# Gated recurrence and bilinear feed-forward: blocks of four token tiles, two PSUM banks for the up-projections

## The chip, the cores and the metric

One core of a Trainium2 chip runs the whole program in one launch. The metric is the device time of one execution in microseconds (us), lower being better. The core's engines are called here by the profile's names: PE (TensorE, the matmuls; its loading of weights is shown as PEld), DVE (VectorE), ACT (ScalarE), POOL (GpSimd) and SP (SyncE, whose queue issues the DMAs). TensorE writes its results to PSUM, which has eight banks; a bank holds 512 float32 values in each of 128 partitions.

## The reference

There are 4 sequences (B), 8 heads (H), 768 steps (S) and 40 values per head (D). For each step and head a matrix state C and a vector state n are updated under two gates with a running maximum, and read with q. The result is the input x of a bilinear feed-forward layer: 3072 tokens, 320 wide, 1536 inner columns, everything in float32.

```python
m_new = np.maximum(f_gate[:, :, t] + m, i_gate[:, :, t])
f_stab = np.exp(f_gate[:, :, t] + m - m_new)
i_stab = np.exp(i_gate[:, :, t] - m_new)
C = f_stab[..., None, None] * C + i_stab[..., None, None] * np.einsum('bhd,bhe->bhde', vt, kt)
n = f_stab[..., None] * n + i_stab[..., None] * kt
h_tilde = np.einsum('bhde,bhe->bhd', C, qt)
denom = np.maximum(np.abs(np.einsum('bhd,bhd->bh', n, qt)), 1.0)[:, :, None]
y[:, :, t] = sigmoid(o_gate[:, :, t]) * h_tilde / denom
...
x = y.transpose(0, 2, 1, 3).reshape(B * S, H * D)
out = ((x @ w_a) * (x @ w_b)) @ w_out
```

## The kernel before

**Attention.** The recurrence is computed in chunks of 128 steps, so there are 24 tiles of 128 tokens, six for each sequence; tile n is chunk n // 4 of sequence n % 4. For a tile, `stage_a` (or `begin_a`) turns q and k so that heads lie along partitions, `stage_e`/`begin_e` make the matrix of gate factors, `stage_b` multiplies it with the scores (PSUM tile pS), `stage_i` reads the state left by earlier chunks (pI), `stage_c` applies the weights to v (pV), `stage_u` updates the state (pU), `stage_f` divides and applies the output gate, and `stage_d` transposes the result (pX) and leaves it as x in two parts: xh, the value rounded to the matmul's format, and xl, what the rounding left. Tiles 0 to 5 use the float32 forms (`begin_...`), the others sums of bfloat16 parts.

**Feed-forward.** `moe_block` takes a block of consecutive tiles together. For each of 12 slices of 128 inner columns (ff), `up` fills two PSUM accumulators, acc[0] = x w_a and acc[1] = x w_b, with eight matmuls each (three parts of the contraction; high and low parts of weights and of x). The matmuls are as wide as the block: 128 columns a tile (L693). ACT copies acc[0] to g (L699; DVE does it in slices 1 and 2), DVE multiplies acc[1] by g (L700), rounds the product to gh (L702), and gl is what the rounding left (L704). `down(ff)` adds gh and gl times w_out into one PSUM accumulator pd for each tile, three matmuls a tile (L664), and runs two slices behind `up`: in a block's first two slices no `down` stands between the `up`s. Behind the last slice ACT copies each pd to o (L673), and SP sends it out (L674). g and o are tiles of one kind, "acp", with three buffers.

**Weights.** The weights arrive as raw 64-bit words. `weights` converts them in 32 stages; `first` makes a high word W and a remainder r with ACT and DVE, and `second` adds them exactly with two matmuls into a PSUM tile pc (L352, L353), from which DVE makes the low part (L354). A block's projections can't run ahead of the stage that they use (`need`). The conversion ends within block 0.

**PSUM.** Three banks "pu" serve acc, and also pc, the gate scores pE of the first tiles and half of the first transposes pT; three banks pd0 to pd2 serve the down-projections (pd2 also pU of tiles 2 to 5, while blocks have two tiles); two banks "pat" serve attention.

**Order.** Each engine works off its instructions in the order in which they are queued. A scheduler sets that order when the program is built, from the order in which the program names the instructions, from simulated times and from the buffers that are free. The program names attention's steps between the projections' matmuls: while block kb is projected, the loop at the end advances attention until the last tile of block kb+1 is done, in steps of a pace (`units / total`). Block 0 may begin when tiles 0 and 1 are done, and each block when all of its tiles are.

The numbers of lines are those of the kernel before.

Of the kernel before, what the change touches and what calls it, by code (L numbers as in the profile page):

```python
# [8 lines left out]
F32 = mybir.dt.float32  # L9
BF16 = mybir.dt.bfloat16  # L10
F32R = mybir.dt.float32r
# [5 lines left out]
PSUM = bass.MemoryType.PSUM  # L17
# [3 lines left out]
def kernel(  # L21
# [14 lines left out]
    B, H, S, D = q.shape  # L36
    DM, DFF = w_a.shape
    P = 128
    NC = S // P
    NF = DFF // P  # L40
    BH = B * H
    DV = D + 2
    TB = 3
    NTB = TB * P
    WCH = 384
    CVB = 8
    STAGES = 8

    BEHIND = ((0, ("k", 0)), (1, ("k", 1)), (14, ("k", 2)), (22, ("k", 3)))
    NF32 = 6  # L50
# [4 lines left out]
    rpool = ctx.enter_context(tc.tile_pool(name="rpool", bufs=1))  # L55
    apool = ctx.enter_context(tc.tile_pool(name="apool", bufs=2))
    dpool = ctx.enter_context(tc.tile_pool(name="dpool", bufs=1, space=bass.MemoryType.DRAM))
    ps_up = ctx.enter_context(tc.tile_pool(name="ps_up", bufs=3, space=PSUM))
    ps_dn = ctx.enter_context(tc.tile_pool(name="ps_dn", bufs=1, space=PSUM))
    ps_at = ctx.enter_context(tc.tile_pool(name="ps_at", bufs=2, space=PSUM))  # L60

# [18 lines left out]
    HH = H // 2  # L80
# [33 lines left out]

    chunks = [(c, b) for c in range(NC) for b in range(B)]
    NCH = len(chunks)
    sizes = [2, 2, 3, 3, 3, 3, 3, 2, 3]
    NB = len(sizes)
    begins = [sum(sizes[:x]) for x in range(NB + 1)]
    assert begins[-1] == NCH and max(sizes) <= TB  # L120
# [61 lines left out]
        return x.bitcast(BF16).rearrange("p h (d w) -> p h d w", w=2)[:, :, :, 1]  # L182

    def gates():
        f = room("g_f")[0:BH, 0:S]
        i = room("g_i")[0:BH, 0:S]
        nc.sync.dma_start(f, f_gate.rearrange("b h s -> (b h) s"))
        nc.sync.dma_start(i, i_gate.rearrange("b h s -> (b h) s"))
        m = room("g_m")[0:BH]
        gb = m[:, S:].rearrange("p (w t) -> p w t", w=2)  # L190
        m = m[:, 0:S]
        yield
# [114 lines left out]
    def weights():  # L307
        stages = list(weight_stages())
        held = {}

        def fetch(x):
            if x < len(stages):
                src = stages[x]
                n = src[0].shape[1]
                raw = rpool.tile([P, n], I64, tag=f"s{x}", name=f"raw{x}")
                r0 = 0
                behind = [y for first, y in BEHIND if x >= first][-1]
                with tc.issue_after(issued[behind]), tc.issue_after(issued.get("w", issued[behind])):
                    for a in src:
                        raw_in = nc.sync.dma_start(raw[r0:r0 + a.shape[0]], a).ins  # L320
                        r0 += a.shape[0]
                issued["w"] = raw_in
                held[x] = [raw, n]

        def first(x):
            raw, n = held[x]
            W = cpool.tile([P, WCH], F32, tag="cv", name="cw", bufs=CVB)[:, :n]
            t = step[x % len(step)][:, :n]
            words = raw.bitcast(U32).rearrange("p (n w) -> p n w", w=2)
            lo, hi = words[:, :, 0], words[:, :, 1]  # L330
            wu, tu = W.bitcast(U32), t.bitcast(U32)


            nc.scalar.activation(t, hi.bitcast(F32), AF.Prelu, scale=2.0 ** -112, alpha=-(2.0 ** 32))
            nc.vector.tensor_scalar(wu, tu, 3, None, op0=ALU.logical_shift_left)
            nc.vector.tensor_scalar(tu, wu, 0xFF800000, None, op0=ALU.bitwise_and)
            r = cpool.tile([P, WCH], F32R, tag="cv", name="cr", bufs=CVB)[:, :n]
            nc.vector.scalar_tensor_tensor(r, lo, 2.0 ** -52, t, op0=ALU.mult, op1=ALU.mult)
            held[x] += [W, r]

        def second(x):

            ready[0] = x + 1
            raw, n, W, r = held.pop(x)
            w = ws[x] = rpool.tile([P, 2, n], F32R, tag=f"s{x}", name=f"w{x}")
            h, l = w[:, 0], w[:, 1]
            last = len(stages[x]) > 1
            if last:
                h, l = (cpool.tile([P, WCH], F32R, tag="ct", name="ct", bufs=2) for _ in range(2))
            nc.scalar.copy(h, W)  # L350
            pc = ps_up.tile([P, NTB], F32, tag="pu", name=f"pc{x}")[:, :n]
            nc.tensor.matmul(pc, eye[0], r, start=True, stop=False)  # L352
            nc.tensor.matmul(pc, eye[1], h, start=False, stop=True)  # L353
            nc.vector.tensor_tensor(l, pc, W, op=ALU.add)  # L354
            if last:
                for j in range(2):
                    rows, other = (slice(64 * i, 64 * i + 64) for i in (j, 1 - j))
                    nc.sync.dma_start(w[rows, j].bitcast(F32), h[rows].bitcast(F32))
                    nc.sync.dma_start(w[other, j].bitcast(F32), l[rows].bitcast(F32))

        fetch(0)
        yield -1
        for x in range(1, 4):
            fetch(x)
        for x in range(len(stages) + 1):
            fetch(x + 4)
            if x < len(stages):
                first(x)
                yield x
            if x > 0:  # L370
                second(x - 1)
                yield x
        for x in qks2:
            for w in range(2):
                nc.gpsimd.memset(x[:, w, :, 3 * D:], 0.0)
# [208 lines left out]
        yield  # L584

    xt = {}

    def stage_d(n):
        s = st.pop(n)
        k_ = block[n]  # L590
        t0 = (n - begins[k_]) * P
        if t0 == 0:
            xt[k_] = (
                mpool.tile([P, 3, NTB], F32R, tag="xh", name=f"xh{k_}", bufs=2),
                mpool.tile([P, 3, NTB], F32R, tag="xl", name=f"xl{k_}", bufs=2),
            )
        xh, xl = xt[k_]
        pX = ps_at.tile([P, 512], F32, tag="pat", name=f"pX{n}")
        for t in range(3):
            nc.tensor.transpose(pX[:, t * P:(t + 1) * P], s["y"][:, t * P:(t + 1) * P], ident)  # L600
        yield
        px = pX[:, 0:3 * P].rearrange("p (a t) -> p a t", a=3)
        cols = slice(t0, t0 + P)
        after["a"] = [nc.scalar.copy(xh[:, :, cols], px).ins]
        nc.vector.tensor_tensor(
            xl[:, :, cols], px, xh[:, :, cols].bitcast(F32), op=ALU.subtract
        )
        yield ("done", n)
# [108 lines left out]
    def begin_e(n):  # L717
# [3 lines left out]
        E = E.rearrange("p (h t) -> p h t", h=H)  # L721
        st.setdefault(n, {})["E"] = E
        for hf in range(2):
            tag = "pu"
            pE = (ps_up if tag == "pu" else ps_at).tile([P, HH, P], F32, tag=tag, name=f"pE{n}_{hf}")
            for x in range(HH):
                one_hot = sel[:, b * H + hf * HH + x:b * H + hf * HH + x + 1].broadcast_to([3 * BH, P])
                nc.tensor.matmul(pE[:, x], one_hot, stk[:, 0], start=True, stop=False)
# [5 lines left out]
    def begin_a(n):  # L734
# [5 lines left out]
        for j in range(2):  # L740
# [3 lines left out]
                t = apool.tile([P, 2 * H * P], BF16, tag=f"T{j}", name=f"T{n}_{j}", bufs=1).bitcast(F32)  # L744
                t = t[:, 0:HH * P].rearrange("p (h t) -> p h t", h=HH)
            T.append(t)
            tag = "pu" if n < NS and j == 1 else "pat"
            pT = (ps_up if tag == "pu" else ps_at).tile([P, 512], F32, tag=tag, name=f"pT{n}_{j}")
            pt = pT.rearrange("p (h t) -> p h t", h=HH)
            for x in range(HH):  # L750
                nc.tensor.transpose(  # L751
# [73 lines left out]

    cpool = ctx.enter_context(tc.tile_pool(name="cpool", bufs=1))
    conv = weights()
    with tc.tile_pool(name="spool", bufs=7) as spool:

        def room(name):  # L830
            return spool.tile([P, H * P], F32, tag="x", name=name)
# [62 lines left out]
    for kb in range(NB):  # L894
# [1 line left out]
        done = False  # L896
        acc = 0.0
        total = NF * (16 + 3 * sizes[kb])
        units = 36 * sizes[kb + 1] if kb + 1 < NB and kb < 2 else 66 * TB
        for x, _ in enumerate(moe_block(kb)):  # L900
            if x % 6 == 0:
                next(conv, None)
# [38 lines left out]
```

## Time and profile before

| | |
|---|---|
| median of 3 runs | 578.44 us (574.6, 578.44, 578.54) |
| span of the profiled execution, first to last instruction | 572.6 us |
| the profiled execution's own time | not given beside its span |
| busy: PE, PEld | 96%, 92% |
| busy: DVE, ACT, POOL | 69%, 46%, 23% |
| granted PE clock, mean | 0.973 |

From the records of L693, 192 for each block, the blocks begin at these times (us from the span's start):

| block | 0 | 1 | 2 | 3 | 4 | 5 | 6 | 7 | 8 |
|---|---|---|---|---|---|---|---|---|---|
| tiles | 2 | 2 | 3 | 3 | 3 | 3 | 3 | 2 | 3 |
| begins | 47.5 | 128.4 | 168.3 | 233.1 | 295.0 | 356.5 | 418.1 | 476.3 | 518.1 |

How to read it: a busy share is of the whole span, and the blocks differ. A matmul's duration in the profile contains its way through the array, so matmuls overlap, and how fast they follow each other is read from their starts. "[1.28 <-DMA out_dram<-o]" behind a row of the order-of-time view says that the engine was idle for 1.28 us before it, and what came last of what it waited for; "x3" says that three instructions in a row were merged.

### The profile page before, as it was taken

To read this page: it belongs to the slowest core of one execution; us is meant where nothing else is said; L and a number is where in the kernel's file an instruction comes from. 1 tells how busy PE (TensorE), PEld (TensorE's weight loads), DVE (VectorE), ACT (ScalarE), POOL (GpSimd) and SP (SyncE) were. 2 spreads that over 40 slices of the span, in tenths; PEclk is the share of its full clock that TensorE was granted. 3 is DMA by queue.
4 is the path that set the end of the run, shared out by engine and by line. 5 is a ranking of instruction groups with operands and counts; after the bars stand their busy time and mean duration, and the time that the engine had idled before them with its cause. 6 is when DMAs were issued, how large, how long until landed. Compare 5 with 4: busy or idle time off the path is not lost.

```text
span 572.6 us, 12609 instructions
## 1 busy us (share of the span) xinstructions
PE 547.5 (96%) x4864; PEld 526.0 (92%) x4864; DVE 396.8 (69%) x884; ACT 265.9 (46%) x634; POOL 129.1 (23%) x182
## 2 busy tenths in 40 slices
PE   3799999999999999999999999999999999999997
PEld 2688999889999989999999999999999899999996
DVE  6866788975578777499649976698648654954342
ACT  3644565673255465255825554555525921411111
POOL 3021331463213222123303330332111200200000
PEclk9857999989999999999999999999999999999999
DMA  9979945365244966267954676478538603200000
GB/s 206 285 184 278 228 111 107 73 153 121 63 103 115 190 118 142 75 123 148 155 109 110 150 150 131 115 159 159 109 97 129 154 2 99 59 2 23 1 2 34
DMA packets 199863, 68.34 MB, mean 119 GB/s; under 512 B 184476, under 2 KB 193084, under 8 KB 199804
## 3 DMA queue, kind: packets, MB, share of 16 engines
q1 hardware_dynamic: 199804, 67.55, 54.6%
q8 instruction: 38, 0.62, 0.5%
q14 instruction: 21, 0.17, 0.1%
HBM read 41.11 MB, written 5.97 MB: 82 GB/s over the span
## 4 chain that ended last, share of the span: by engine, by line
PE 85%; DVE 4%; ACT 4%; DMA 3%; issue 1%; SPq 1%; POOL 1%; ACTq 0%; DVEq 0%; POOLq 0%
PE pu L693 45%; PE pd L664 21%; PE pV L503 4%; PE pU L527 3%; PE pS L451 3%; PE pV L807 2%; PE pS L764 2%; PE pX L600 2%; PE pI L477 1%; PE pc L352 1%; DMA qk<-in_k_dram 1%; PE pT L751 1%; ACT gbc L396 1%; DMA T<-qks 1%; DMA gbc<-g_dram 1%
## 5 line engine op out<-in xcount | busy, mean ns | idle before, releaser
L693 PE MATMUL pu<-xh,w 128*128 128x384 f32 (+1 forms) x1080 | 278.1, 325 | 2.8 <-ACT g L699 1.9
L693 PE MATMUL pu<-xl,w 128*128 128x384 f32 (+1 forms) x648 | 208.4, 323 | 0.0
L693 PEld LDWEIGHTS pu<-xh,w 128*128 128x128 f32 x1080 | 192.0, 190 | 5.3 <-ACT g L699 2.9
L664 PE MATMUL pd<-w,gh 128*128 128x320 f32 x576 | 127.2, 311 | 0.0
L700 DVE TENSOR_TENSOR g<-pu,g 128x384 f32<-128x384 f32 (+1 forms) x108 | 54.9, 508 | 100.3 <-ACT g L699 51.6
L693 PEld LDWEIGHTS pu<-xl,w 128*128 128x128 f32 x648 | 123.2, 190 | 0.1
L664 PEld LDWEIGHTS pd<-w,gh 128*128 128x128 f32 x576 | 97.2, 189 | 0.3
L664 PE MATMUL pd<-w,gl 128*128 128x320 f32 x288 | 85.8, 312 | 0.0
L699 ACT COPY g<-pu 128x384 f32<-128x384 f32 (+1 forms) x90 | 39.6, 440 | 95.1 <-PE pu L693 88.3
L396 ACT ACTIVATE gbc<-gbc,gtab 128x128 f32<-128x128 f32 x160 | 49.1, 389 | 16.3 <-POOL gbc L389 16.2
L664 PEld LDWEIGHTS pd<-w,gl 128*128 128x128 f32 x288 | 53.1, 189 | 0.1
L704 DVE TENSOR_TENSOR gl<-g,gh 128x384 fp32r<-128x384 f32 (+1 forms) x92 | 50.6, 550 | 2.1
L493 POOL TENSOR_TENSOR vw<-va,gtab 128x336 f32<-128x336 f32 x14 | 10.8, 769 | 161.7 <-PE pU L527 139.0
L702 DVE CAST gh<-g 128x384 fp32r<-128x384 f32 (+1 forms) x108 | 41.2, 382 | 2.4
L389 POOL TENSOR_SCALAR_AFFINE_SELECT gbc<-gbc 128x1024 f32<-128x1024 f32 x20 | 23.9, 1197 | 61.6 <-DMA va<-in_v_dram 33.2
L579 POOL TENSOR_TENSOR osig<-osig,den 128x320 f32<-128x320 f32 x24 | 19.6, 816 | 65.0 <-DVE den L574 45.8
L418 DVE TENSOR_TENSOR r<-qk,qks 128x320 f32<-128x320 f32 x36 | 18.0, 502 | 19.8 <-ACT qks L414 17.0
L414 ACT CAST qks<-qk 128x320 bf16<-128x320 f32 x36 | 16.3, 452 | 31.2 <-DMA T<-qks 27.7
L673 ACT COPY o<-pd 128x320 f32<-128x320 f32 x24 | 8.8, 434 | 42.9 <-PE pd L664 42.9
L424 ACT COPY qks<-qks 128x640 bf16<-128x640 bf16 x36 | 26.0, 726 | 0.4
L460 DVE TENSOR_TENSOR gbc<-gbc,pb 128x512 f32<-128x512 f32 x36 | 24.5, 704 | 2.3 <-ACT pb L458 2.0
L456 DVE TENSOR_TENSOR gbc<-pS,gbc 128x512 f32<-128x512 f32 x36 | 23.6, 679 | 3.3 <-PE pS L451 3.3
(133 smaller groups left out, 878.9 us busy)
## 6 DMA issues: line engine op xcount, KB each, us to landing
gbc<-g_dram SPq DMA_DIRECT2D x20, 512.0 KB
va<-in_v_dram SPq DMA_DIRECT2D x24, 160.0 KB
qk<-in_q_dram SPq DMA_DIRECT2D x24, 160.0 KB
qk<-in_k_dram SPq DMA_DIRECT2D x24, 160.0 KB
osig<-in_o_gate_dram SPq DMA_DIRECT2D x24, 160.0 KB
raw<-in_moe_w_out_dram SPq DMA_DIRECT2D x12, 320.0 KB
out_dram<-o SPq DMA_DIRECT2D x24, 160.0 KB
raw<-in_moe_w_a_dram SPq DMA_DIRECT2D x8, 384.0 KB
```

Of the source, the lines that this page charges most:

```text
L389: nc.gpsimd.affine_select(E, E, pattern=[[0, H], [1, P]], compare_op=ALU.is_ge, fill=-1e30, base=0, channel_multiplier=-1,)
L396: nc.scalar.activation(E[:, h], E[:, h], AF.Exp, bias=beta[:, h:h + 1])
L424: nc.scalar.copy(qks[:, 0, :, lo:lo + 2 * D], qks[:, 1, :, D - lo:3 * D - lo])
L456: nc.vector.tensor_tensor(E, pS, E, op=ALU.mult)
L460: nc.vector.tensor_tensor(E, E, pb[:, 0], op=ALU.subtract)
L503: nc.tensor.matmul(pv[:, h], pb[i][:, h % HH, :], vb[j][:, h], start=(x == 0), stop=(x == len(terms) - 1),)
L664: nc.tensor.matmul(pd[t][:, 0:DM], a[:, cols], w, start=(ff == 0 and first), stop=(ff == NF - 1 and last),)
L693: nc.tensor.matmul(acc[j], a, r, start=(x == 0), stop=(x == len(terms) - 1),)
L699: (nc.vector.tensor_copy if ff in [1, 2] else nc.scalar.copy)(g, acc[0])
L700: nc.vector.tensor_tensor(g, acc[1], g, op=ALU.mult)
L702: nc.vector.tensor_copy(gh, g)
L704: (nc.gpsimd if kb * 12 + ff < 16 else nc.vector).tensor_tensor(gl, g, gh.bitcast(F32), op=ALU.subtract)
```

## The change

Blocks behind the first two have four tiles, so that an up-projection's matmul has 512 columns and fills a bank; there are seven blocks in place of nine. A fourth bank for down-projections, pd3, is taken from the up-projections' three. What else used those three moves: pc and half of the first pT to pd3, the pE of tiles 2 and 3 to pd2. x has a pool of its own with two rooms for xh and two for xl, 128 x 1536 values each. The first pair holds the gates before it holds the x of blocks 0 and 1; the second holds W and r of the conversion, four stages of each, before it holds x of block 2; later blocks alternate. Before, W and r took turns in eight buffers of their own, and the gates lay in rooms of the pool for the start. The pace of attention in blocks 0 and 1 now follows which tiles are of the float32 kind.

```diff
-    TB = 3
+    TB = 4
...
-    CVB = 8
...
-    ps_up = ctx.enter_context(tc.tile_pool(name="ps_up", bufs=3, space=PSUM))
+    ps_up = ctx.enter_context(tc.tile_pool(name="ps_up", bufs=2, space=PSUM))
...
-    sizes = [2, 2, 3, 3, 3, 3, 3, 2, 3]
+    sizes = [2, 2, 4, 4, 4, 4, 4]
...
-        f = room("g_f")[0:BH, 0:S]
-        i = room("g_i")[0:BH, 0:S]
+        both = xpool.tile([P, 3 * NTB], F32, tag="xl", name="g_fi")[0:BH]
+        f, i = both[:, 0:S], both[:, S:]
+        m = xpool.tile([P, 3 * NTB], F32, tag="xh", name="g_m")[0:BH, 0:H * P]
...
-        m = room("g_m")[0:BH]
...
+        rings = []
+
+        def scratch(x, j):
+            if not rings:
+                rings.append(xpool.tile([P, 3 * NTB], F32, tag="xl", name="cw"))
+                rings.append(xpool.tile([P, 3 * NTB], F32R, tag="xh", name="cr"))
+            x = x % (3 * NTB // WCH) * WCH
+            return rings[j][:, x:x + WCH]
...
-            W = cpool.tile([P, WCH], F32, tag="cv", name="cw", bufs=CVB)[:, :n]
+            W = scratch(x, 0)[:, :n]
...
-            r = cpool.tile([P, WCH], F32R, tag="cv", name="cr", bufs=CVB)[:, :n]
+            r = scratch(x, 1)[:, :n]
...
-            pc = ps_up.tile([P, NTB], F32, tag="pu", name=f"pc{x}")[:, :n]
+            pc = ps_dn.tile([P, 512], F32, tag="pd3", name=f"pc{x}")[:, :n]
...
-            xt[k_] = (
-                mpool.tile([P, 3, NTB], F32R, tag="xh", name=f"xh{k_}", bufs=2),
-                mpool.tile([P, 3, NTB], F32R, tag="xl", name=f"xl{k_}", bufs=2),
-            )
+            if k_ != 1:
+                parts = [xpool.tile([P, 3 * NTB], F32R, tag=x, name=f"{x}{k_}") for x in ("xh", "xl")]
+            if k_ == 0:
+                first.extend(parts)
+            if k_ < 2:
+                xt[k_] = tuple(x.rearrange("p (k a t) -> p k a t", k=2, a=3)[:, k_] for x in first)
+            else:
+                xt[k_] = tuple(x.rearrange("p (a t) -> p a t", a=3) for x in parts)
...
-            tag = "pu"
-            pE = (ps_up if tag == "pu" else ps_at).tile([P, HH, P], F32, tag=tag, name=f"pE{n}_{hf}")
+            pool, tag = (ps_up, "pu") if n < NS else (ps_dn, "pd2")
+            pE = pool.tile([P, HH, P], F32, tag=tag, name=f"pE{n}_{hf}")
...
-            tag = "pu" if n < NS and j == 1 else "pat"
-            pT = (ps_up if tag == "pu" else ps_at).tile([P, 512], F32, tag=tag, name=f"pT{n}_{j}")
+            pool, tag = (ps_dn, "pd3") if n < NS and j == 1 else (ps_at, "pat")
+            pT = pool.tile([P, 512], F32, tag=tag, name=f"pT{n}_{j}")
...
+    xpool = ctx.enter_context(tc.tile_pool(name="xpool", bufs=2))
-    with tc.tile_pool(name="spool", bufs=7) as spool:
+    with tc.tile_pool(name="spool", bufs=3) as spool:
...
-        units = 36 * sizes[kb + 1] if kb + 1 < NB and kb < 2 else 66 * TB
+        units = 66 * TB
+        if kb < 2:
+            units = sum(36 if n < NF32 else 66 for n in range(begins[kb + 1], begins[kb + 2]))
```

More of the change, by code (lines that the diff above doesn't have):

```diff
@@ L586 @@
     xt = {}
+    first = []
     def stage_d(n):
```

## The prediction

> **What bounds the kernel now.** I read the page of the profile first, then the busy time of each engine in the stretch of each block (a block's stretch begins with its first up-projection matmul), then what TensorE waited for.
>
> ```profile
> span 572.6 us, 12609 instructions
> PE 547.5 (96%) x4864; PEld 526.0 (92%) x4864; DVE 396.8 (69%) x884; ACT 265.9 (46%) x634; POOL 129.1 (23%) x182
> PEclk9857999989999999999999999999999999999999
> PE 85%; DVE 4%; ACT 4%; DMA 3%; issue 1%; SPq 1%; POOL 1%; ACTq 0%; DVEq 0%; POOLq 0%
> L693 PE MATMUL pu<-xh,w 128*128 128x384 f32 (+1 forms) x1080 | 278.1, 325 | 2.8 <-ACT g L699 1.9
> L693 PE MATMUL pu<-xl,w 128*128 128x384 f32 (+1 forms) x648 | 208.4, 323 | 0.0
> ```
> ```profile
> 47.50:128.40 80.90, 78.33 (x597) 72.72 (x596) 65.44 (x163) 47.92 (x117) 28.86 (x40) 0.93 0.66 152
> 128.40:168.30 39.90, 39.90 (x409) 38.93 (x408) 26.22 (x62) 16.59 (x43) 10.13 (x13) 1.00 0.47 104
> 295.00:356.50 61.50, 61.50 (x599) 59.69 (x598) 47.97 (x101) 32.51 (x79) 16.63 (x21) 1.00 0.62 134
> 518.10:572.60 54.50, 50.43 (x308) 50.17 (x306) 18.60 (x39) 6.54 (x15) 0.00 (x0) 1.00 0.05 16
> ```
> ```profile
> PE pu L693 <- ACT g L699: 1.9, 3, 0.7
> ```
>
> The columns of the second fence are the stretch, its length, and busy time of PE, PEld, DVE, ACT and POOL, then granted clock and DMA. From the second block on (128 us) TensorE has hardly a hole: 39.90 of 39.90, 61.50 of 61.50. DVE, next, is at 26.22/39.90 = 66% and 47.97/61.50 = 78%. The third fence is all that TensorE waited for an up-projection bank behind 128 us: 1.9 us in three waits. So TensorE's issue sets the end, and a change is worth what it takes out of that issue or puts into it as holes. The profile gives the span, 572.6 us, and no other time of that execution; the runs' median, 578.44 us, is 5.8 us above it. I put the sum, a difference, on the median. 1% is also 5.8 us, and about what this kernel's measurement can tell from no change.
>
> **Part 1: fewer, longer up-projection matmuls.** 1080 + 648 = 1728 matmuls of L693 are 192 for each of nine blocks. Busy time of a matmul contains its latency, so I take start to start, from the order-of-time view:
>
> ```profile
> 511.65 0.28 PE L693 MATMUL pu<-xh,w 128*128 128x256 f32 x1
> 512.61 0.31 PE L664 MATMUL pd<-w,gh 128*128 128x320 f32 x1
> ```
> ```profile
> 560.30 0.45 PE L664 MATMUL pd<-w,gh 128*128 128x320 f32 x2
> 561.61 0.34 PE L693 MATMUL pu<-xh,w 128*128 128x384 f32 x1
> 564.42 0.31 PE L664 MATMUL pd<-w,gh 128*128 128x320 f32 x1
> ```
>
> Eight matmuls of 256 columns lie between the first two rows: 0.96/8 = 0.120 us each. Nine of 320 columns take 561.61 - 560.30 = 1.31, 0.1456 each; sixteen of 384 take 2.81, 0.1756 each. From 256 to 384 that is 0.0556 us per 128 columns, so 512 columns cost 0.231, and some 0.009 us of each matmul does not depend on its width. Up-projections now: 3 blocks x 192 x 0.120 + 6 x 192 x 0.1756 = 271.4 us. After: 2 x 192 x 0.120 + 5 x 192 x 0.231 = 267.8. **-3.6 us.** Bounds: by the slope between 256 and 320 (0.0256 per 64) 512 columns cost 0.2268, -7.6 us; by that between 320 and 384 (0.030 per 64) 0.2356, +0.9 us. I take the middle since it spans both. The Trainium skill, "TensorE: Matmul & The Clock Gate", section "Back-to-back issue gap", puts a warm gap at N/2.4 ns plus 2.5; 384 matmuls fewer would by that save 1.0 us, an estimate from that page, and the sum below would end 2.6 us higher. The rows show a larger fixed part than it states. Down-projections (three per tile and slice) and the attention keep their counts.
>
> **Part 2: two banks at a block's start.** With three banks the second round's acc[0] has a bank of its own. With two it needs the bank that the copy g of the first round empties (L699), and that copy stands on ACT's queue behind the copies o of the block before (L673), which wait for its last down-projections. g and o also share the three buffers "acp". Two block starts, the three-tile one first:
>
> ```profile
> 297.69 1.09 ACT L673 COPY o<-pd 128x320 f32<-128x320 f32 x3 [2.53 <-PE pd L664]
> 297.93 0.34 PE L693 MATMUL pu<-xl,w 128*128 128x384 f32 x1
> 298.14 1.33 SPq L674 DMA_DIRECT2D out_dram<-o  x3
> 299.34 0.34 PE L693 MATMUL pu<-xl,w 128*128 128x384 f32 x1
> 300.05 0.48 ACT L699 COPY g<-pu 128x384 f32<-128x384 f32 x1 [1.28 <-DMA out_dram<-o]
> ```
> ```profile
> 520.91 0.59 PE L664 MATMUL pd<-w,gh 128*128 128x320 f32 x3
> 521.69 0.75 ACT L673 COPY o<-pd 128x320 f32<-128x320 f32 x2 [5.70 <-PE pd L664]
> 521.78 0.34 PE L693 MATMUL pu<-xh,w 128*128 128x384 f32 x1
> 522.33 0.50 ACT L699 COPY g<-pu 128x384 f32<-128x384 f32 x1
> ```
>
> In the first, three o fill the three buffers, and g starts 300.05 - 297.69 = 2.36 us after the first o, when that one's output has left. Four tiles make a fourth o, which takes that buffer at +2.36 and ACT for 0.36 (1.09/3); g gets the second buffer one issue later (1.33/3 = 0.44), at +2.80, and ends near +3.4 (0.48 us, at most 4/3 of it). TensorE goes on with acc[1] at 297.93, +0.24, for 8 x 0.231 = 1.85, and then stands from +2.1 to +3.4: 1.3 us. In the second order both accumulators run ahead of the last down-projections, and TensorE would stand from 521.78 to the end of g, 522.83: 1.05 us with two o; with four, from about +0.3 to +3.4, 3.1 us. I give the starts of blocks 3, 4 and 5 the first order (3 x 1.3), block 6, with no attention beside it, the second (3.1), and blocks 1 and 2, behind two-tile blocks, 1.05 each: 3.9 + 3.1 + 2.1 = 9.1. Where attention is there, its matmuls can fill such holes; I take half of those 6.0 away. **+6.1 us**, between 0 (g is queued ahead of o everywhere) and 4 x 3.1 + 2.1 = 14.5.
>
> **Part 3: two banks inside a block.** ACT is now and then held by attention's work:
>
> ```profile
> 214.69 0.43 PE L693 MATMUL pu<-xl,w 128*128 128x384 f32 x1
> 217.68 0.34 PE L693 MATMUL pu<-xh,w 128*128 128x384 f32 x1
> 219.69 0.34 PE L693 MATMUL pu<-xl,w 128*128 128x384 f32 x1
> 220.75 0.44 PE L693 MATMUL pu<-xh,w 128*128 128x384 f32 x1 [0.72 <-ACT g L699]
> ```
> ```profile
> 217.53 2.45 ACT L396 ACTIVATE gbc<-gbc,gtab 128x128 f32<-128x128 f32 x8 [2.24 <-POOL gbc L389]
> 220.23 0.46 ACT L699 COPY g<-pu 128x384 f32<-128x384 f32 x1
> ```
>
> The accumulator whose last matmul is at 214.69 was emptied by 220.69. The next round's acc[0] began at 217.68 in the third bank, and only acc[1] waited, at 219.87. With two banks acc[0] waits, 3.0 us earlier in the order. Four tiles give back 8 x 0.055 of longer acc[1] and 3 x 0.146 more of down-projection, 0.9 us: 2.1 instead of today's 0.9. There are three such waits: 3 x 1.2. DVE's multiply (L700), which frees the other bank, follows the same copies and I add nothing for it. **+3 us**; bounds 0 and 6.3 (three of 2.1, and none of today's falls away).
>
> **Part 4: the end.** Four o for three buffers:
>
> ```profile
> 568.27 1.08 ACT L673 COPY o<-pd 128x320 f32<-128x320 f32 x3 [4.57 <-PE pd L664]
> 568.73 1.30 SPq L674 DMA_DIRECT2D out_dram<-o  x3
> ```
>
> The last o ends 1.08 us after the first begins; the fourth would begin at +2.36 and end at +2.7: **+1.5 us**, with 0.1 off for an earlier first. Nothing hides it.
>
> **Part 5: the rest, at nothing.** The conversion's sums (L352 to L354) go from the shared banks to one of their own, so each waits for DVE's addition of the one before; the gate scores of tiles 2 and 3 go to the bank of pU, their second halves waiting for ACT's exponential of the first. Behind them on TensorE stand projections of the first block. There it is busy 78.33 of 80.90 us; the holes, 2.6 us, are what this could gain, and as much again I allow as a loss. The transposes of k of the first two tiles change banks ahead of all projections. x of later blocks waits for rooms whose readers ended a block earlier; the conversion keeps four stages in flight. If that cover is gone, it is the late tile below. The same 24 tiles' loads and stores pass SP's queue.
>
> **Sum:** -3.6 + 6.1 + 3 + 1.5 = +7.0; 578.44 + 7.0 = **585.4 us**. Own range, by the bounds of part 2: 579 to 594.
>
> **Rivals.** *Filled holes:* the order is worked out anew with two banks, and attention's matmuls take all holes that have any beside them. Left: -3.6, block 6's 3.1, the end's 1.5, 1 inside: +2, 580.4 us. For it: today's TensorE is never idle with attention beside it. Against: g stands behind o at both starts shown.
>
> *Faster:* g is queued ahead of o, and the first block gets rid of its holes because conversion and projection no longer share banks.
>
> ```profile
> 108.00:113.00 5.00, 3.76 (x29) 3.53 (x29) 5.00 (x13) 1.98 (x6) 2.16 (x3) 0.98 0.02 6
> 113.00:120.00 7.00, 7.00 (x32) 7.00 (x32) 6.01 (x18) 3.71 (x9) 2.92 (x7) 0.53 0.64 161
> ```
>
> After a hole of 1.24 us the clock falls to 0.53 for 7 us, 7 x 0.47 = 3.3 us lost. -3.6 - 1.2 - 3.3 + 1.5 = -6.6: 571.8 us. It decides where no wait on g remains at block starts. Against: DVE is busy all 5.00 us of that hole, so banks are not what was lacking.
>
> *The fourth tile comes late:* block 2 can't begin before tile 7's x.
>
> ```profile
> 164.51 0.55 DVE L605 TENSOR_TENSOR xl<-pX,xh 128x384 fp32r<-128x384 f32 x1
> 188.59 0.56 DVE L605 TENSOR_TENSOR xl<-pX,xh 128x384 fp32r<-128x384 f32 x1
> ```
>
> These are tiles 6 and 7. A tile's attention is 4 us of TensorE: 61.50 less 192 x 0.1756 and 108 x 0.1456, over three tiles. So block 1 would end near 168.3 + 4 + 1 of holes = 173; had tile 7 kept its 189.1, TensorE would idle 16 us. For it: DVE, at 66% of this stretch, gets another tile's work. Against: today the written pace asks for tile 7 only in block 2, and will ask for it in block 1. It costs as soon as that row ends behind 173; with 10 us, 595 us.
>
> *The clock falls at each hole:* as at 113 us, 3.3 us for each of four starts, 13 more, 598 us. Against: the hole at 219.87 left no trace in the clock row. The Trainium skill has this as a rule, "TensorE: Matmul & The Clock Gate", section "A second HAM failure mode: psum-queue depth-cycling": small idles from cycling through PSUM banks make the clock go to and fro.
>
> **Numbers.** Forecast 0.46, filled holes 0.22, faster 0.16, late tile 0.11, clock 0.05. Slower by over 1% (from 584.2) is 0.28 of the forecast's 0.46 plus 0.11 and 0.05: 0.44. Faster is 0.16. The rest, 0.40, is within 1%. The range reaches from the faster case to the late tile: 572 to 595.
>
> **What would show it.** 1344 matmuls of L693's successor, 0.231 apart at 512 columns. Waits of pu on ACT's g, and on the multiply, of 9 us or so instead of 1.9, most of them in a block's first round; o waiting for its own output's DMA. Wrong if starts of blocks show no hole, if 512 columns cost under 0.227 or over 0.236, or if block 2 begins with a wait for xl.

## The result, and the profile after

On the chip of the first comparison the changed kernel took 583.62 us (median of 4 runs, 581.77 to 585.77), the kernel before 576.62 us (4 runs, 574.6 to 578.54). The ratio is 1.0138, with a 95% interval of 1.0091 to 1.0184: **slower by 1.4%**. Some executions run in a slower state, which the ratios leave out and the medians don't: one of four of two_banks and of two_own below, and a few of the kernel before. The profiled execution's own time is 583.52 us, 1.7 us above its span of 581.8. Every other profiled execution with a time on record lies 1.8 to 1.9 us above its span, so the one before, span 572.6 us, took some 574.4 us (an estimate), about the lowest of its runs. That is why the spans below differ by 9.2 us and the medians by 7.0.

The page of the changed kernel: summary, clock row, shares of the chain that ended last, the up-projections' two groups and the copies o. In a group's line, "busy, mean ns of one" is followed by the idle time before it and what ended most of that.

```profile
span 581.8 us, 11712 instructions
PE 549.2 (94%) x4480; PEld 482.1 (83%) x4480; DVE 390.6 (67%) x808; ACT 263.8 (45%) x614; POOL 129.3 (22%) x182
PEclk9757999979999999999999999999999999989998
...
PE 79%; ACT 5%; DVE 4%; SPq 4%; DMA 3%; issue 3%; POOL 1%; ACTq 0%; POOLq 0%; DVEq 0%
L705 PE MATMUL pu<-xh,w 128*128 128x512 f32 (+1 forms) x840 | 254.2, 371 | 8.3 <-ACT g L711 5.2
L705 PE MATMUL pu<-xl,w 128*128 128x512 f32 (+1 forms) x504 | 183.7, 365 | 0.0
L685 ACT COPY o<-pd 128x320 f32<-128x320 f32 x24 | 9.1, 432 | 39.7 <-PE pd L676 33.3
```

There are 840 + 504 = 1344 up-projections, and TensorE's instructions fell from 4864 to 4480. Yet the span grew by 581.8 - 572.6 = 9.2 us, and the chain now runs through TensorE for 79% of the span where it was 85%. Waits for g (L711, L699 before) rose from 1.9 to 5.2 us. The clock row has a new 8 in its fifth slice from the end.

Blocks 0, 1, 3 and 6 of the seven, and what TensorE waited for (columns of the first fence: stretch, length, busy time of PE, PEld, DVE, ACT, POOL, granted clock, DMA share, GB/s; the second is cut to three rows):

```profile
51.70:133.90 82.20, 76.72 (x595) 69.21 (x594) 68.09 (x163) 49.01 (x123) 29.26 (x42) 0.95 0.73 164
133.90:183.50 49.60, 47.57 (x526) 43.94 (x522) 33.44 (x76) 25.07 (x62) 14.39 (x19) 1.00 0.68 137
...
262.90:344.90 82.00, 81.81 (x735) 71.09 (x734) 61.82 (x119) 43.70 (x101) 23.01 (x28) 1.00 0.63 132
505.00:581.80 76.80, 68.65 (x349) 59.91 (x348) 23.48 (x39) 8.89 (x18) 0.00 (x0) 0.96 0.05 18
```
```profile
PE pu L705 <- ACT g L711: 5.2, 6, 2.6
PE pc L359 <- DVE w L361: 3.3, 5, 1.0
...
PE pu L705 <- DMA w<-ct: 3.0, 1, 3.0
```

In the middle (block 3) TensorE is busy 81.81 of 82.00 us, as it was before. The holes lie at the two ends of the program: in blocks 0 and 1, and in the last one.

To say where the 9.2 us came from, I set against each block's length what its matmuls would take at the pace of undisturbed rows. That pace is read from start to start: 0.120 us for 256 columns, 0.1745 for 384, 0.146 for the 320 of a down-projection, and 0.229 for 512, for which this round of the last block stands:

```profile
563.55 0.39 PE L705 MATMUL pu<-xh,w 128*128 128x512 f32 x1
...
567.20 0.89 PE L676 MATMUL pd<-w,gh 128*128 128x320 f32 x5
```

Sixteen matmuls lie between the two starts: 3.65/16 = 0.228. Every other form of matmul has its own distance from start to start. A block's length less the sum is "lost", whether TensorE stood, ran at half clock or issued more slowly. The differences between the columns change by up to some 1.5 us with the distance taken for attention's small matmuls, and the losses of the start and of block 0 themselves by much more; how the 4.1 us divide between these two is not settled by it. The lines add up to 9.1 for rounding.

| lost, us | before | changed | difference |
|---|---|---|---|
| matmuls at their undisturbed pace, all | 510.8 | 506.5 | -4.3 |
| start and block 0 | 44.4 | 48.5 | +4.1 |
| block 1 (two tiles) | 1.3 | 6.9 | +5.6 |
| the blocks between (six; four) | 11.8 | 9.7 | -2.1 |
| last block | 0.1 | 4.4 | +4.3 |
| behind the last matmul | 4.2 | 5.7 | +1.5 |
| span | 572.6 | 581.8 | +9.2 |

The last block's loss, in order of time, on PE and then on ACT:

```profile
510.23 0.31 PE L676 MATMUL pd<-w,gl 128*128 128x320 f32 x1
513.17 0.51 PE L705 MATMUL pu<-xh,w 128*128 128x512 f32 x1 [2.63 <-ACT g L711]
514.81 1.06 PE L705 MATMUL pu<-xh,w 128*128 128x512 f32 x2
515.67 0.63 PE L705 MATMUL pu<-xl,w 128*128 128x512 f32 x1
```
```profile
509.69 1.08 ACT L685 COPY o<-pd 128x320 f32<-128x320 f32 x3 [7.66 <-PE pd L676]
512.04 0.42 ACT L685 COPY o<-pd 128x320 f32<-128x320 f32 x1 [1.26 <-DMA out_dram<-o]
512.53 0.58 ACT L711 COPY g<-pu 128x512 f32<-128x512 f32 x1
```

Three copies o fill the three buffers. The fourth waits 1.26 us until the first one's output has left, and g is queued behind it; TensorE, out of banks, stands from the down-projection at 510.23 to 513.17. Then two matmuls take 515.67 - 514.81 = 0.86 us, 0.43 each instead of 0.229: the clock was halved.

### The profile page after: what moved, and what is told of

Its sections match the earlier page's. It is cut to its first block, busy times and chain, and to the rows that moved or that the text cites. A ratio compares the mean times of both kernels' runs of the same rounds, so it can differ in the third digit from the quotient of the medians.

```text
span 581.8 us, 11712 instructions
## 1 busy us (share of the span) xinstructions
PE 549.2 (94%) x4480; PEld 482.1 (83%) x4480; DVE 390.6 (67%) x808; ACT 263.8 (45%) x614; POOL 129.3 (22%) x182
## 4 chain that ended last, share of the span: by engine, by line
PE 79%; ACT 5%; DVE 4%; SPq 4%; DMA 3%; issue 3%; POOL 1%; ACTq 0%; POOLq 0%; DVEq 0%
PE pu L705 42%; PE pd L676 19%; PE pV L510 3%; PE pU L534 3%; PE pS L458 2%; PE pS L776 2%; PE pV L819 2%; ACT gbc L403 1%; SPq L164 1%; PE pX L612 1%; DMA out_dram<-o 1%; PE pc L359 1%; SPq L327 1%; PE pI L484 1%; DMA raw<-in_moe_w_b_dram 1%
## 5 line engine op out<-in xcount | busy, mean ns | idle before, releaser
L705 PE MATMUL pu<-xh,w 128*128 128x512 f32 (+1 forms) x840 | 254.2, 371 | 8.3 <-ACT g L711 5.2
L705 PE MATMUL pu<-xl,w 128*128 128x512 f32 (+1 forms) x504 | 183.7, 365 | 0.0
L705 PEld LDWEIGHTS pu<-xh,w 128*128 128x128 f32 x840 | 153.6, 191 | 33.5 <-ACT g L711 7.2
L712 DVE TENSOR_TENSOR g<-pu,g 128x512 f32<-128x512 f32 (+1 forms) x84 | 51.0, 607 | 85.7 <-PE pu L705 63.0
L705 PEld LDWEIGHTS pu<-xl,w 128*128 128x128 f32 x504 | 96.3, 191 | 11.3 <-DVE xl L617 0.4
L711 ACT COPY g<-pu 128x512 f32<-128x512 f32 (+1 forms) x70 | 36.4, 521 | 94.0 <-PE pu L705 93.5
L716 DVE TENSOR_TENSOR gl<-g,gh 128x512 fp32r<-128x512 f32 (+1 forms) x68 | 47.6, 700 | 1.4
L714 DVE CAST gh<-g 128x512 fp32r<-128x512 f32 (+1 forms) x84 | 38.9, 464 | 1.5
L517 DVE TENSOR_TENSOR num<-pV,num 128x336 f32<-128x336 f32 x18 | 9.1, 504 | 29.2 <-PE pV L510 29.0
L510 PEld LDWEIGHTS <-pb 128*128 128x128 bf16 x576 | 23.6, 96 | 4.9 <-issue 3.3
```

The costliest lines, as they stand in the source:

```text
L510: nc.tensor.matmul(pv[:, h], pb[i][:, h % HH, :], vb[j][:, h], start=(x == 0), stop=(x == len(terms) - 1),)
L705: nc.tensor.matmul(acc[j], a, r, start=(x == 0), stop=(x == len(terms) - 1),)
L711: (nc.vector.tensor_copy if ff in [1, 2] else nc.scalar.copy)(g, acc[0])
L712: nc.vector.tensor_tensor(g, acc[1], g, op=ALU.mult)
L714: nc.vector.tensor_copy(gh, g)
L716: (nc.gpsimd if kb * 12 + ff < 16 else nc.vector).tensor_tensor(gl, g, gh.bitcast(F32), op=ALU.subtract)
```

## The experiments

The first theory was the prediction's mechanism: what the change costs is waits for an up-projection bank at block starts, with g behind o. The rivals put the loss in the conversion's and the start's shared banks, or spread it over all rounds. The kernels ran in three groups, each beside the kernel before on its own chip; ratios are to that, with 95% intervals.

**Own buffers for o** (o_own). The copies o leave the kind "acp" and get four buffers.

```diff
-                    o = mpool.tile([P, NTB], F32, tag="acp", name=f"o{kb}_{t}")[:, 0:DM]
+                    o = mpool.tile([P, DM], F32, tag="ot", name=f"o{kb}_{t}", bufs=4)
```

> The changed kernel, but the output copies o get four buffers of their own in place of three shared with g. Theory 1 (the loss sits at the last block's start, at the end and at the program's start): the last block's hole of 2.9 us, the fall of the clock behind it (1.7 us) and 1.3 us of the end go: 5 to 6 us faster than the changed kernel's 583.6, about 578. Theory 2 (two banks cost a little in every round of every block): only the end's 1.3 us go, about 582.3.

576.81 us (10 runs) beside 573.95: 1.0074 (1.0032 to 1.0115). Start of the last block, ACT and then PE, and the end:

```profile
510.37 0.59 ACT L711 COPY g<-pu 128x512 f32<-128x512 f32 x1 [4.82 <-PE pu L705]
513.06 1.41 ACT L685 COPY o<-pd 128x320 f32<-128x320 f32 x4 [2.10 <-PE pd L676]
...
574.77 1.41 ACT L685 COPY o<-pd 128x320 f32<-128x320 f32 x4 [4.34 <-PE pd L676]
```
```profile
513.59 0.31 PE L676 MATMUL pd<-w,gl 128*128 128x320 f32 x1
513.74 0.39 PE L705 MATMUL pu<-xh,w 128*128 128x512 f32 x1
```

The hole of 2.94 us from start to start has become one matmul's distance, 0.15, and the last block loses -0.1 us instead of 4.4. The reason is more than the wait for a buffer: g is now queued *ahead* of o. The scheduler sets a queue's order also by the buffers that are free, and with no shared kind nothing held g back. At the end four o follow each other without a pause; behind the last matmul 4.4 us are left instead of 5.7. The mechanism of the last block and of the end is shown; whether a kind of their own or the fourth buffer did it for g was not separated. Beside the changed kernel's 1.4 to 1.8% above the kernel before, 0.7% is 4 to 6 us gained, about what theory 1 expected. The profiled execution took 581.16 us, 4.4 above its median, so what its start shows is not typical.

**Half of the first transposes back to "pu"** (pt_back).

```diff
-            pool, tag = (ps_dn, "pd3") if n < NS and j == 1 else (ps_at, "pat")
+            pool, tag = (ps_up, "pu") if n < NS and j == 1 else (ps_at, "pat")
```

> The changed kernel, but the second half of the first two tiles' transposes pT goes to the up-projections' banks, as before the change; the conversion's sums pc stay alone in pd3. Theory 1 (pc waits 3.2 us for DVE's copy of pT out of pd3, and all of the program's start with it): block 0 begins near 48 us instead of 51.7, 3 to 4 us faster, about 580. Rival (the start is late for another reason, such as the gates' rooms): within 1 us of 583.6, block 0 near 51.7.

584.06 us (4 runs): 1.0179 (1.0107 to 1.0250). Block 0 begins at 52.2 us, where the changed kernel's begins at 51.7. The transposes' place in pd3 is not what delays the start; it is refuted.

**The conversion's sums back to "pu"** (pc_back).

```diff
-            pc = ps_dn.tile([P, 512], F32, tag="pd3", name=f"pc{x}")[:, :n]
+            pc = ps_up.tile([P, NTB], F32, tag="pu", name=f"pc{x}")[:, :n]
```

> The changed kernel, but the conversion's sums pc share the up-projections' two banks, and pT keeps pd3. Theory 1: the start gains its 3 to 4 us as in the run with pT moved back, and block 0 loses up to that much again, since each sum takes one of only two banks from the projections: 583.6 with 3 us either way. Rival (one bank is what holds the conversion back; waits of pc on DVE's sum, 3.3 us, and the late last weights, 3.0 us, go too): 5 us or more faster, under 579.

585.34 us (4 runs): 1.0189 (1.0115 to 1.0263). Block 0 begins at 51.1 and is 83.3 us long, no shorter than the changed kernel's 82.2. There the sums share two banks with the projections, and one trouble replaces the other:

```profile
PE pu L705 <- ACT g L711: 5.2, 5, 2.6
PE pX L612 <- DVE num L798: 4.3, 1, 4.3
...
PE pc L359 <- ACT gbc L743: 3.0, 1, 3.0
```

The waits of pc on L361 are gone from these rows, but a transpose pX now waits 4.3 us, and pc waits 3.0 us for a reader of the gate scores. There is no gain.

**Two banks alone** (two_banks): the kernel before with its blocks of two and three tiles, the third bank "pu" taken away, and pE, pT and pc placed as the change places them (here without a need, since no fourth tile uses pd3).

```diff
-    ps_up = ctx.enter_context(tc.tile_pool(name="ps_up", bufs=3, space=PSUM))
+    ps_up = ctx.enter_context(tc.tile_pool(name="ps_up", bufs=2, space=PSUM))
```

> The kernel before with its blocks of two and three tiles, but two banks for up-projections; pc and half of pT go to a free bank pd3, pE of tiles 2 and 3 to pd2, as in the changed kernel. Theory 1: the start's 4 us and about 1 us at the last block's start, nothing inside blocks: 5 us above the kernel before, about 582. Theory 2: eight block starts at 1.1 to 1.3 us and lags inside blocks on top, 15 us or more above, over 591.

612.11 us (4 runs): 1.0622 (1.0514 to 1.0730). That is some 36 us by the ratio, about four times what the whole change costs (6.2% against 1.4 to 1.8%). It is not the price of two banks alone, since the conversion's sums also got a single bank here. The first theory, which bound the price to block starts, fell with this run.

**Two banks, and own buffers for o** (two_own): as before, with three buffers of o's own. **The changed kernel again** (after_same), as the level of that chip.

```diff
-                    o = mpool.tile([P, NTB], F32, tag="acp", name=f"o{kb}_{t}")[:, 0:DM]
+                    o = mpool.tile([P, DM], F32, tag="ot", name=f"o{kb}_{t}", bufs=3)
```

> Blocks of two and three tiles with two banks, as in the run two_banks (612 us, 38 above before), and three buffers of their own for o. Theory A (with two banks the first copy g of a block is what TensorE waits for, since it is queued behind o, at eight block starts): 8 to 12 us faster than two_banks, about 602. Theory B (what two banks cost is spread over the rounds, since three tiles give each round too little cover): within 4 us of two_banks.

> The changed kernel as it is, again, to stand on the same chip beside the others of this group. No edit: 7 us (1.2%) above the kernel before, as first measured, by every theory.

two_own: 609.80 us (4 runs), 1.0562 (1.0450 to 1.0674), 2 to 4 us less than without. after_same: 584.82 us (4 runs), 1.0178 (1.0109 to 1.0247). So o is not the main price here. Blocks 0, 3 and 4 of two_own and one place in block 3, then that place on PE, and what TensorE waited for most in block 0:

```profile
48.50:147.20 98.70, 88.25 (x591) 80.48 (x590) 68.63 (x171) 51.31 (x126) 30.69 (x43) 0.83 0.62 146
252.60:321.50 68.90, 64.99 (x613) 61.86 (x612) 47.46 (x99) 33.54 (x79) 16.16 (x21) 0.98 0.62 120
321.50:384.10 62.60, 62.60 (x594) 59.75 (x592) 47.93 (x99) 32.56 (x78) 16.37 (x21) 1.00 0.64 132
302.00:306.00 4.00, 1.07 (x15) 0.71 (x10) 1.25 (x3) 4.00 (x13) 0.52 (x1) 1.00 0.15 40
```
```profile
302.81 0.30 PE L664 MATMUL pd<-w,gl 128*128 128x320 f32 x1
306.37 0.45 PE L693 MATMUL pu<-xh,w 128*128 128x384 f32 x1 [3.26 <-ACT g L699]
```
```profile
PE pu L693 <- DMA w<-ct: 7.2, 4, 2.4
```

Block 4 has no hole, block 3 has one of 3.6 us, far from its ends (302 of 252.6 to 321.5). There ACT is busy all of 4.00 us with attention's work, and g stands behind it. That is part 3 of the prediction, but in a block of three tiles. Behind this hole the clock is at half for 3.4 us, which is another 1.7 us of that block's loss. Block 0 is the larger part: 98.7 us long against 80.9 before, 18 us more. Two things are on record for it. TensorE stands for 98.70 - 88.25 = 10.5 us instead of 2.6, mostly for converted weights (7.2 us; a further 2.0 us are pc's waits for its one bank). And the clock is at half for 34 us of the block instead of 11, at most 17 us lost instead of 5. In two_banks it is the same: 9.0 us idle, 34 us at half. So much of the price in block 0 comes by way of the conversion and of the clock, and not by a wait for g.

**Other sizes** (sizes8): o_own with blocks of 2, 2, 3, 3, 4, 4, 4 and 2 tiles.

```diff
-    sizes = [2, 2, 4, 4, 4, 4, 4]
+    sizes = [2, 2, 3, 3, 4, 4, 4, 2]
```

> The changed kernel with o in four buffers of its own, and eight blocks of 2, 2, 3, 3, 4, 4, 4, 2 tiles: block 1 carries the attention of three tiles, as before, not four. Theory A (the fourth tile's attention makes block 1 lose 5 us): 5 less 1.7 for 192 more up-projection matmuls, 3 us faster than o_own, about 573. Theory B (two banks need four tiles for cover; the blocks of three tiles lose 4 to 6 us each more, as in two_banks): 6 us or more slower, over 582.

589.73 us (4 runs): 1.0265 (1.0172 to 1.0357), against o_own's 1.0074. The 192 matmuls more are 2.1 us of the 11 (508.6 instead of 506.5 us at the undisturbed pace). The two three-tile blocks lose 4.6 and 5.8 us (1.7 of the latter is a fall of the clock behind a wait for g of 1.89 us), two of the three four-tile blocks behind them 4.2 and 4.7, the third under 1; o_own's four-tile blocks with attention lost 1.7 to 3.3. Blocks of three tiles do worse on two banks, but they aren't the whole of it. A four-tile block waits for g too, here in block 4:

```profile
368.59 0.50 PE L705 MATMUL pu<-xh,w 128*128 128x512 f32 x1 [1.50 <-ACT g L711]
```

Theory A fell: block 1, with the attention of three tiles, is 44.0 us long, where the kernel before's, also with three, is 39.9. By the sum of matmuls it loses some 4 us, o_own's with four tiles some 5 and the kernel before's 1.3. The fourth tile is the smaller part of block 1's loss.

**Two banks for the conversion's sums** (pc_two): o_own, with pc in turn in pd2 and pd3.

```diff
-            pc = ps_dn.tile([P, 512], F32, tag="pd3", name=f"pc{x}")[:, :n]
+            pc = ps_dn.tile([P, 512], F32, tag=f"pd{2 + x % 2}", name=f"pc{x}")[:, :n]
```

> The changed kernel with o in four buffers of its own (run o_own), and the conversion's sums pc in turn in pd2 and pd3 instead of in pd3 alone. Theory A (one bank for pc holds up TensorE in the start and in block 0; o_own waits 2.9 us there for DVE to empty it): 3 us or more faster than o_own, about 573, waits of pc on DVE's sum under 1 us. Theory B (these waits stand in for others, as in pt_back, where the copy of pT was taken off pd3 and the start was as late): within 2 us of o_own.

575.45 us (10 runs) beside 573.85: 1.0035 (1.0000 to 1.0069), and 9.4 us below the changed kernel on the same chip. The end of the conversion in the changed kernel, on PE:

```profile
119.06 0.42 PE L359 MATMUL pc<-cr,eye 128*128 128x320 f32 x1 [0.93 <-DVE ct L361]
...
120.59 0.41 PE L359 MATMUL pc<-cr,eye 128*128 128x320 f32 x1 [0.96 <-DVE w L361]
...
124.17 0.58 PE L705 MATMUL pu<-xh,w 128*128 128x256 f32 x1 [3.02 <-DMA w<-ct]
```

The second addition has no bank until DVE has read the first (L361), twice, and behind that the projections wait 3.02 us for the last converted weights. In pc_two none of these three waits is left in block 0, which is 78.1 us long instead of 82.2 and by the sum of matmuls loses 14.1 us, about as before the change (14.3). The holes are shown to go with the bank. What that is worth in time is less sure: o_own and pc_two differ by 0.4%, and their intervals overlap.

**A third bank in block 1** (bank3): pc_two, and in block 1, whose two tiles leave pd3 unused, every third accumulator lies there.

```diff
-                ps_up.tile([P, NTB], F32, tag="pu", name=f"pu{kb}_{ff}_{j}")[:, 0:NT]
+                (ps_dn.tile([P, 512], F32, tag="pd3", name=f"pu{kb}_{ff}_{j}")
+                 if kb == 1 and (2 * ff + j) % 3 == 2 else
+                 ps_up.tile([P, NTB], F32, tag="pu", name=f"pu{kb}_{ff}_{j}"))[:, 0:NT]
```

> The run pc_two, and in block 1 the up-projections take turns in three banks, the third being pd3, which is free there (conversion is over, block 1 has two tiles). Theory A (block 1's loss against the kernel before, 5 to 6 us, is the missing bank: its largest hole in pc_two, 2.4 us, is a wait for g): 2.5 to 4 us faster than pc_two, 572, at or under the kernel before. Theory B (block 1 loses to the fourth tile's attention and its DMAs): within 1.5 us of pc_two.

572.12 us (12 runs) beside 574.69: 0.9937 (0.9906 to 0.9968). **By these ratios this version beats both kernels.** Block 1 of pc_two, its largest hole on ACT and PE, the stretch behind it, and then the two largest waits of bank3's TensorE from block 1 to the end:

```profile
172.52 2.44 ACT L403 ACTIVATE gbc<-gbc,gtab 128x128 f32<-128x128 f32 x8 [4.16 <-POOL gbc L396]
174.87 0.35 ACT L711 COPY g<-pu 128x256 f32<-128x256 f32 x1
```
```profile
175.27 0.39 PE L705 MATMUL pu<-xh,w 128*128 128x256 f32 x1 [2.23 <-ACT g L711]
```
```profile
176.20:179.60 3.40, 3.40 (x21) 3.20 (x20) 3.40 (x8) 2.41 (x6) 0.00 (x0) 0.50 0.82 162
```
```profile
PE pd L676 <- ACT o L685: 1.5, 1, 1.5
PE pu L707 <- ACT g L713: 1.0, 2, 0.5
```

In pc_two eight exponentials hold ACT for 2.44 us, g starts behind them, and TensorE stands for 2.23 us; then the clock is at half for 3.4 us (1.7 us lost). In bank3 no wait on g is longer than 0.5 us, the clock stays up, and block 1 loses 4.2 instead of 7.0 us, which is still more than the 1.3 of the kernel before. That the third bank as such is worth this is not shown. Blocks 1 and 2 have the same tiles in all kernels of this shape; together they last 129.5 us in bank3 and 132.0 in pc_two, but on two banks 129.0 in the changed kernel and 128.2 in o_own, with 1 to 2 us less of attention's matmuls in them than in bank3. These two were laid out without so large a hole there. Nor does block 1 account for all of the 1% between pc_two and bank3.

**Own buffers for o in the kernel before** (three_own), to see whether o_own's edit is worth something by itself. Its edit is that of two_own, on the kernel before.

> The kernel before, with three buffers of their own for o. With three banks no round waits for a block's first g, so by every theory within 1.5 us of the kernel before; a larger gain would mean that the gain of own buffers in four-tile blocks has little to do with the two banks.

575.81 us (12 runs): 1.0020 (0.9991 to 1.0048). Nothing is gained with three banks. What bank3 has over the kernel before doesn't come from this edit alone.

**The price of a matmul** (split): pc_two with each 512-column up-projection as two of 256, 960 matmuls more for the same sums.

```diff
-                    nc.tensor.matmul(
-                        acc[j], a, r, start=(x == 0), stop=(x == len(terms) - 1),
-                    )
+                    for c0 in range(0, NT, 256):
+                        nc.tensor.matmul(
+                            acc[j][:, c0:c0 + 256], a, r[:, c0:c0 + 256],
+                            start=(x == 0 and c0 == 0), stop=(x == len(terms) - 1 and c0 + 256 >= NT),
+                        )
```

> The run pc_two, but each 512-column up-projection matmul is issued as two of 256 into the halves of the same bank: 960 matmuls more, the same columns. If each matmul carries a fixed part that sits on TensorE's issue (start to start 0.120 us at 256 columns, 0.229 at 512), 960 x (0.240 - 0.229) = 10.6 us slower than pc_two, 586. If that part is hidden or belongs to the wide form, within 3 us of pc_two.

595.38 us (4 runs): 1.0351 (1.0289 to 1.0414), some 18 to 20 us above pc_two, where 10.6 were expected. The last block, pc_two's and then split's:

```profile
502.40:569.00 66.60, 66.60 (x350) 58.77 (x348) 23.50 (x39) 7.44 (x15) 0.00 (x0) 1.00 0.03 11
```
```profile
519.60:588.50 68.90, 68.90 (x541) 68.81 (x539) 23.08 (x38) 7.47 (x15) 0.00 (x0) 1.00 0.03 10
```

Without attention beside them 192 matmuls more cost 2.3 us, 12 ns each; five such blocks make 12 us. The rest of the 18 to 20 lies where attention runs: blocks 2 to 5 grew by 8.6, 4.4, 4.8 and 3.2 us. In block 2 a wait for g of 2.04 us, with the clock at half for 6.8 us behind it (3.4 lost), makes up most of what goes beyond 2.3. The weight loads have no slack left in the last block (68.81 of 68.90 us). That the loads are why attention's matmuls fit in worse elsewhere was not tested.

## Why the prediction was right or wrong

The forecast was +7.0 us; measured were +7.0 us by the medians of the first comparison and +11.0 us in the second. The total was right, and in part by luck. The matmuls (-3.6), the last block (3.1) and the end (1.5) came out near -4.3, 4.3 and 1.5. But the start and blocks 0 and 1, put at half a microsecond by parts 2 and 5, lost 9.7 more, and the blocks between, put at some 5.5 by parts 2 and 3, lost 2.1 less: two errors against each other.

- **Part 1, fewer matmuls: right.** -3.6 forecast; -4.3 by the table's first line. 512 columns took 0.228 to 0.229 us, not 0.231, and 384 took 0.1745, not 0.1756. split confirms the part of a matmul that does not depend on its width: 12 ns from a whole block, where the prediction's rows gave 9. The Trainium skill's 2.5 ns ("TensorE: Matmul & The Clock Gate", section "Back-to-back issue gap"), which that page gives for the isolated gap of one matmul and not for a stream of weight loads and matmuls as here, would by an estimate have made the last block of split 192 x 0.0025 = 0.5 us longer; it was 2.3.
- **Part 2, block starts: right for the last block, too dear in the middle, and one size missing.** The last block was put at 3.1 us: its hole is 2.94 from start to start, with the order of ACT that was foretold, the fourth o behind its buffer. Undoing it (o_own) removes it. Missing was the clock, which took another 1.7 us of that block's 4.4. It is a small piece of the clock rival: once, not at four starts. Blocks 3 to 5, put at 1.3 each and then halved, show almost nothing: all waits on g between 183.5 and 505 us come to 1.6 us, 0.6 of them at block 2's start. There the rival of filled holes was the better account.
- **Part 3, inside blocks: the mechanism exists, the place and the number were wrong.** (Its sum has a slip: 3 x 1.2 is 3.6, entered as 3.) Attention's work on ACT does hold g up and TensorE with it, but hardly in the changed kernel: blocks 2 to 5, sixteen tiles, lost 9.7 us, where before the blocks 2 to 7, seventeen tiles, lost 11.8, and apart from the last block's start no wait on g is longer than 0.8 us. The step that failed took three waits of today's order and made each 2.1 us long. The order was laid out anew, and such a wait falls where a hold of ACT happens to meet it: 2.23 us in block 1 of pc_two, 3.26 us in block 3 of two_own, 1.50 and 2.04 us in four-tile blocks of sizes8 and split, nowhere in the changed kernel. By the pace of the rows a round of 16 up- and 3 down-projections a tile lasts 16 x 0.229 + 12 x 0.146 = 5.4 us with four tiles, 16 x 0.120 + 6 x 0.146 = 2.8 us with two, so the same hold of ACT is a smaller share of it. That long rounds are therefore less sensitive is argued from these sums; sizes8 and split bear it out only in part. In block 1 of the changed kernel TensorE is idle for 49.60 - 47.57 = 2.0 of the 6.9 us that it lost; the rest is spread over its matmuls, and no wait names it.
- **Part 4, the end: right.** +1.5 forecast, +1.5 measured; o_own takes 1.3 of it back.
- **Part 5, the rest at nothing: wrong.** It named the step itself, "each waits for DVE's addition of the one before", and priced it at zero with 2.6 us as the bound. Start and block 0 lost 4.1 us more. In block 0, 0.93 + 0.96 + 3.02 = 4.9 us are the conversion's waits in the one bank and the projections' wait for what it delivers. They go when the sums get a second bank (the kernel before loses some in the same place, so not all of the 4.9 is new). Why the cover failed is argued, not shown: these sums come last in the conversion, when block 0 has little else that may run. The first block begins some 4 us later in every kernel made from the changed one (51 to 54 us against 46 to 48.5 of those made from the kernel before); some 2 to 4 us of that, by the distance taken for small matmuls, is matmul work that now comes ahead of it, above all gate scores pE. For the rest neither the place of pT nor that of pc is the cause, nor the clock: two_banks begins block 0 at 48.5 with 27 us at half clock ahead of it, the changed kernel at 51.7 with 26. The new rooms for the gates and the conversion's words were not tried alone. That stays open.
- **The rivals.** "Faster" asked that g be queued ahead of o; the changed kernel doesn't do that, but own buffers for o bring it about. The late fourth tile didn't happen: block 2 begins behind a wait for g, not for xl. "Wrong if starts of blocks show no hole" came true for blocks 3 to 5, and the forecast's waits of about 9 us were 5.2, none of them on the multiply.

Open also is why block 0 is 17 to 18 us longer in the kernels with three-tile blocks on two banks (two_banks, two_own) and hardly longer in the changed one, though pc has a single bank in all three: TensorE's waits and the half clock there are on record, what brought them is not. Each edit makes the scheduler lay the order out anew, and builds that differ in one tile's place differ by several microseconds in the start and in block 0.

## What to carry to other kernels

When a resource is taken from a ring (three banks to two), price it by how long the other engine is held up, and don't trust the places where it meets a wait today, since a new order moves them: holds of ACT of over 2 us cost 1.5 to 3.3 us in some of these kernels, in blocks of two, three and four tiles, and under 1 us in others. The clock behind such a wait comes on top. Three repairs together (own buffers for o, a second bank for the conversion's sums, a third bank in the short block) turned a loss of 1.4% into a gain of 0.6%. Buffers of one kind for two uses tie the order of an engine's queue: giving the outputs their own put the urgent copy ahead of them, and the hole was gone. A resource's new single place must be priced by the chain behind it at its last use, not by how busy the stage is on average.

## What was not expected of the hardware

The same hole lowered the clock in one execution and not in another. At the start of the last block TensorE stood for 2.6 us in four profiled executions of three kernels with the same order there. Changed kernel, and its second profile (after_same), the stretches behind the hole:

```profile
512.80:517.80 5.00, 4.63 (x13) 3.72 (x14) 2.50 (x4) 0.32 (x1) 0.00 (x0) 0.66 0.09 33
```
```profile
516.00:520.00 4.00, 3.60 (x16) 3.01 (x17) 2.50 (x4) 0.34 (x1) 0.00 (x0) 1.00 0.12 41
```

In the first the mean granted clock is 0.66, and it was 0.5 for some 3.4 us; in the second it stays at 1.00, and the last block lost 2.8 us instead of 4.4. pt_back has it low (0.60 over 4 us), pc_back has 1.00.

The traces show more than chance. In every profile here the clock changes only in steps of 3.41 us, so the whole time can be cut into such windows, with the edges where the clock changed. These are the windows that hold the hole, in the changed kernel and then in after_same:

```profile
510.60:514.00 3.40, 0.83 (x4) 0.70 (x5) 0.81 (x2) 1.19 (x3) 0.00 (x0) 0.99 0.56 193
```
```profile
511.80:515.20 3.40, 1.97 (x13) 1.67 (x12) 0.00 (x0) 1.08 (x3) 0.00 (x0) 1.00 0.28 94
515.20:518.60 3.40, 2.20 (x10) 1.84 (x11) 1.88 (x4) 1.01 (x2) 0.00 (x0) 1.00 0.29 99
```

In the first the hole lies nearly whole in one window, TensorE is busy for 0.83 of its 3.40 us, and the next window is at half. The edges lie elsewhere in each execution: in the second one cuts the hole in two, neither window is below 1.97, and the clock stays up. The others agree: 1.07 in pt_back and 1.17 in pc_two's block 1 were followed by half, 1.71 in pc_back was not. Busy time alone is not the whole rule: in block 0, with its many small matmuls, windows with over 2 us also had half behind them. That a hole's place in the window decides was not tested by moving one.

The Trainium skill, "TensorE: Matmul & The Clock Gate", section "What's actually happening", puts the fall to half after an idle window of about 3.4 us, and says that the windows run freely, so that what a kernel meets varies. The variation and the 3.4 us at half speed agree. Holes of 2.0 to 2.6 us, shorter than that window, were enough here (2.04 in split). Such a hole should be priced with its clock as a chance: 0 or 1.7 us more.
